# Attention and two MLP layers on one core: rows of maxima read in 8-byte runs, and another step table for the attention

## Chip, cores and metric

The kernel runs on one core of a Trainium2 chip. The metric is the device time of one execution in microseconds (us). TensorE (PE) does the matrix products, its weight loads are listed as PEld; VectorE (DVE), ScalarE (ACT) and GpSimd (POOL) do the work on elements; SyncE (SP) issues nearly all DMAs.

## What is computed

```
q, k, v: (batch 2, heads 8, seq 1152, dim 64) f32
q_pool = q.reshape(B, H, 576, 2, 64).mean(axis=3)
scores = (q_pool @ k^T) / 8 ;  scores -= max over keys
attn   = exp(scores) / (sum over keys + 1e-9)
x      = (attn @ v)  ->  1152 tokens of 512
x      = mish(x @ moe_w_in) @ moe_w_out        # 512 -> 2048 -> 512
out    = elu(x @ moe2_w_in) @ moe2_w_out       # 512 -> 2048 -> 512
```

The four weight matrices come as 64-bit floats; the kernel makes a high and a low 32-bit part of each piece of them.

## The kernel before

**Two stages.** `attention()` goes first, `mlps()` second. The order of all instructions is written out by hand, engine by engine; each engine runs its own list in order, and semaphores hold it where an operand or a buffer is not ready.

**Pairs and units.** The 16 (batch, head) combinations go as eight pairs `n`, the two heads of a pair on partitions 0 to 63 and 64 to 127. The 576 pooled queries of a head are cut in a narrow unit (`c` = 0, queries 0 to 255) and a wide unit (`c` = 1, queries 256 to 575). The 1152 keys are nine key tiles `kt` of 128. One unit and one key tile make one step, so a pair has 18 steps: 0 to 8 for the narrow unit, 9 to 17 for the wide one.

**What a step does.** `qk` (L353 to L366) computes the scores of one key tile, keys on the partitions, queries along the row, for both heads at once: four terms of two matmuls each. Three are products of high and low parts of q and k (`QH`, `QL`, `KH`, `KL`), the fourth (`top`, `unit`) subtracts the query's maximum, held as a row in `tops`. `exp` (L372) on ACT turns the two PSUM banks of scores into `pt`. With a `kt` in the list `two`, two key tiles of the narrow unit share one pair of banks and one ACT instruction of 1024 columns. The score banks are a ring of three double banks, taken in turn by `qk` and by the maxima.

**Maxima.** The maximum of each query is needed ahead of its pair's steps. `peak_mm` (L270 to L293) multiplies with queries on the partitions (L279; L286 for the last 128 keys of all four query tiles; L293 for the last 64 queries of both heads, out of `blk`), `peak` (L295 to L309) reduces each result on DVE, and `top` negates the maxima into `neg`. This is a column with one query per partition. To become a row it goes out to DRAM (`top_out`, L336, tensor `hopm`) and back (`top_in`, L342 and L347) in two parts: first queries 0 to 255, then the rest. Each read of L342 fetches 256 single floats. Only pair 0 takes another way: `flip` transposes on PE (L321).

**Sums and values.** `av` (L443) multiplies a key tile of `pt` with V, a matmul on 128 rows and 64 columns per head, and adds up nine key tiles per unit in one bank. `add` (L383) adds key tiles of `pt` on DVE or POOL, by the table `who`; `total` (L398) sums over the keys with a matrix of ones, one source for each of two tiles of added `pt` and one for each key tile that nobody added. The sums are spilled (L409), go through DRAM (`hop`, L415 and L419), are inverted (L423), come back broadcast over partitions (`pop`, `rb`, L427 and L433), and scale the unit's result (L460), which is split in `XH` and `XL`.

**The table.** `PLAN`, for the last pair `LAST`, and `PREP` for the next pair's loads and maxima give the step of each action: `av` the step of each of the 18 V tiles of a pair (counted from the pair's first step, so a value of 18 or more falls in the next pair), `total` and `chain` the sums, `add` the distance of an addition from its score step. Inside a step the order is: maxima marked even, `qk` and `exp`, maxima marked odd, then `av` with `total`, then ACT, DVE, POOL and SP actions. `weight` gives the steps at which one piece of the first four weight chunks is read and taken apart during each pair; its last action, `rest` (L145), makes the low part.

**MLP stage.** `h_mm` (L178) and `out_mm` (L736) alternate on PE for the rest of the run. The first six units of `h_mm` need tokens of batch 0 only, that is of pairs 0 to 3.

Of the kernel before, what the change touches and what calls it, by code (L numbers as in the profile page):

```python
# [22 lines left out]
def tile_pool_attention_mish_elu_mlp(  # L23
# [20 lines left out]
    P = 128  # L44
# [138 lines left out]
    def attention():  # L183
        with ExitStack() as st:
# [84 lines left out]

            def peak_mm(n, e):  # L270
                t, j = evs(n)[e]
                kw = 512 if n else KB
                if e == 0:
                    stat[n] = ap.tile([P, NQ + 1, 2, 3], F32, tag="stat", name="stat")
                    neg[n] = ap.tile([P, NQ + 1, 2], F32R, tag="neg", name="neg")
                pt = sc[n, e] = take()
                if t < NQ:
                    for h in range(2):
                        nc.tensor.matmul(  # L279
                            pt[:, h, :kw], qh[n][half[h], t * P:(t + 1) * P], kh[n][half[h], j * kw:(j + 1) * kw],  # L280
                            start=True, stop=True,
                        )
                elif t > NQ:
                    for x in range(NQ):
                        for h in range(2):
                            nc.tensor.matmul(  # L286
                                pt[:, h, x * P:(x + 1) * P], qh[n][half[h], x * P:(x + 1) * P], kh[n][half[h], S - P:],
# [23 lines left out]
            def top(n, t0, t1):  # L311
                m, g = stat[n], neg[n] if n else pad[:, :, :, 0]
                nc.vector.tensor_reduce(g[:, t0:t1, :], m[:, t0:t1], axis=AX.X, op=ALU.max, negate=True)
                if t1 == NQ:
                    nc.vector.tensor_reduce(g[:, t1, 0:1], m[:, t1, 0:1], axis=AX.X, op=ALU.max, negate=True)


            def flip(t0, t1):
# [6 lines left out]
                if t0 < NQ:  # L325
                    nc.scalar.copy(tops[0][:, t0 * P:t1 * P], pt[:, :(t1 - t0) * P])
# [4 lines left out]
            def top_out(n, t0, t1):  # L331
                if t0 == 0:
                    hops[n] = dp.tile([P, NQ + 1, 2], F32, tag="hopm", name="hopm")
                e = slice(2 * t0, 2 * t1 + (t1 == NQ))
                hop, g = (x.rearrange("p t h -> p (t h)")[:, e] for x in (hops[n], neg[n]))
                nc.sync.dma_start(out=hop, in_=g.bitcast(F32))  # L336

            def top_in(n, t0, t1):
                hop, row = hops[n], tops[n % 2]
                for h in range(2):  # L340
                    r = h * D
                    nc.sync.dma_start(  # L342
                        out=row[r:r + 1, t0 * P:t1 * P].rearrange("o (t p) -> o t p", p=P).bitcast(F32),
                        in_=hop[:, t0:t1, h].rearrange("p t -> t p").unsqueeze(0),
                    )
                    if t1 == NQ:
                        nc.sync.dma_start(  # L347
                            out=row[r:r + 1, NQ * P:].bitcast(F32), in_=hop[half[h], NQ, 0:1].rearrange("p o -> o p")
                        )
# [25 lines left out]
            ADDS = {1: (0, 0, 1), 3: (1, 2, 3), 4: (0, None, 4), 5: (1, None, 5), 6: (0, None, 6), 7: (1, None, 7)}  # L375
# [99 lines left out]
            def at(s, e, f, *args):  # L475
# [6 lines left out]
                "load_q": [-30, -23],  # L482
                "load_k": [-20, -19],
                "load_v": [-1, 9],
                "pool_q": -20,
                "high_q": -17,
                "high_k": [-17, -15],
                "blk_q": -8,
                "low_q": -9,
                "low_k": [-13, -2],  # L490
                "peak": [-28, -23, -20, -18, -12, -10, -10, -1, 2, 4],
                "top": [[2, 1], [1, 3]],
            }
            PREP[2] = {
                "load_q": [-24, -22],
                "load_k": [-20, -18],
                "load_v": [-3, 0],
                "pool_q": -20,
                "high_q": -18,
                "high_k": [-19, -15],  # L500
                "blk_q": -13,
                "low_q": -13,
                "low_k": [-9, -3],
                "peak": [-28, -24, -23, -19, -11, -10, -9, -1, 1, 4],
                "top": [[2, 1], [1, 3]],
# [376 lines left out]
```

## Time and profile before

| | us |
|---|---|
| median of 3 runs | 634.15 (634.05 to 636.31) |
| profiled execution, its own time | 635.57 |
| span of that execution | 633.8 |
| PE busy | 616.9 (97%) |
| DVE busy | 445.9 (70%) |
| ACT busy | 335.1 (53%) |
| POOL busy | 197.9 (31%) |

The profile gives one execution. Its span runs from the first to the last instruction on the core; the execution's own time is 1.8 us longer, and the median lies 1.4 us below that. Shares of busy time are averages over two stages: POOL is busy for 6.0 of 10 us in most of the attention and hardly at all later.

### The profile page before, as it was taken

What the parts mean: (1) busy time and instruction counts of PE and PEld (TensorE: products, weight loads), DVE (VectorE), ACT (ScalarE), POOL (GpSimd) and SP (SyncE); (2) the same over time, 40 slices, a digit from 0 to 9 for tenths busy, and PEclk for the clock granted to TensorE, in tenths of its full rate; (3) what the DMA queues carried; (4) which work ended last, traced back from release to release, by engine and by line L of the source; (5) the groups of instructions that cost most, each with busy time, mean ns of one, the idle gap of its engine ahead of it and who ended that gap; (6) DMA issues with size and microseconds to landing.
All of it is one profiled execution on the core that took longest, in us unless ns stands there. A gap on an engine that the chain in (4) does not pass through costs nothing.

```text
span 633.8 us, 11509 instructions
## 1 busy us (share of the span) xinstructions
PE 616.9 (97%) x4498; PEld 535.2 (84%) x4498; DVE 445.9 (70%) x705; ACT 335.1 (53%) x675; POOL 197.9 (31%) x191
## 2 busy tenths in 40 slices
PE   5899999999999999999999999999999999999997
PEld 3667676676776689999999999999999999999995
DVE  5868767787787468647548657759878788995453
ACT  3665546555565544434344553456666657664441
POOL 5666565657653511101104323333210101100000
PEclk9999999999999999999999999999999999999999
DMA  4234252442523425223232222222232223300111
GB/s 140 84 99 123 67 134 60 131 111 66 132 64 89 89 76 176 67 67 104 68 97 82 85 71 97 97 70 62 72 99 68 66 68 100 109 25 11 40 51 50
DMA packets 50797, 53.34 MB, mean 84 GB/s; under 512 B 17656, under 2 KB 40248, under 8 KB 50744
## 3 DMA queue, kind: packets, MB, share of 16 engines
q1 hardware_dynamic: 50520, 52.29, 28.6%
q8 instruction: 35, 0.57, 0.4%
q10 hardware_dynamic: 224, 0.33, 0.2%
q14 instruction: 18, 0.15, 0.1%
HBM read 50.14 MB, written 2.47 MB: 83 GB/s over the span
## 4 chain that ended last, share of the span: by engine, by line
PE 86%; DMA 6%; DVE 3%; SPq 2%; issue 1%; ACT 1%; DVEq 0%; ACTq 0%
PE banks L178 32%; PE banks L736 31%; PE banks L363 10%; PE banks L443 8%; DMA top<-hopm 3%; PE banks L279 2%; PE banks L398 2%; DVE stat L300 1%; DMA hopm<-neg 1%; PE banks L293 1%; DVE stat L302 1%; DMA kr<-in_k_dram 1%; SPq L342 1%; DMA raw<-in_moe_w_in_dram 1%; DMA qr<-in_q_dram 1%
## 5 line engine op out<-in xcount | busy, mean ns | idle before, releaser
L178 PE MATMUL banks<-XH,wh 128*128 128x384 f32 x384 | 129.5, 337 | 0.0
L178 PE MATMUL banks<-XL,wh 128*128 128x384 f32 x384 | 129.4, 337 | 0.0
L178 PE MATMUL banks<-XH,wl 128*128 128x384 f32 x384 | 129.4, 337 | 0.0
L123 POOL TENSOR_SCALAR wf<-wf 128x512 f32<-128x512 f32 x64 | 43.6, 682 | 256.2 <-ACT wf L119 225.8
L372 ACT ACTIVATE pt<-banks 128x640 f32<-128x640 f32 (+2 forms) x136 | 88.0, 681 | 63.1 <-PE banks L363 62.7
L300 DVE TENSOR_REDUCE stat<-banks 128x2 f32<-128x1024 f32 (+1 forms) x68 | 77.9, 1171 | 13.2 <-PE banks L279 13.0
L443 PE MATMUL banks<-pt,vr 128*64 128x320 f32 (+1 forms) x576 | 79.6, 414 | 0.0
L178 PEld LDWEIGHTS banks<-XH,wh 128*128 128x128 f32 x384 | 72.0, 188 | 2.3 <-issue 0.5
L178 PEld LDWEIGHTS banks<-XL,wh 128*128 128x128 f32 x384 | 72.0, 188 | 1.8
L178 PEld LDWEIGHTS banks<-XH,wl 128*128 128x128 f32 x384 | 72.0, 188 | 0.0
L690 ACT ACTIVATE gh<-banks 128x384 fp32r<-128x384 f32 x48 | 23.7, 493 | 78.7 <-PE banks L178 78.7
L736 PE MATMUL banks<-gh,wl 128*128 128x384 f32 x192 | 64.5, 336 | 0.0
L736 PE MATMUL banks<-gl,wh 128*128 128x384 f32 x192 | 64.5, 336 | 0.0
L736 PE MATMUL banks<-gh,wh 128*128 128x384 f32 x192 | 64.4, 335 | 0.0
L443 PEld LDWEIGHTS banks<-pt,vr 128*64 128x64 f32 x576 | 37.9, 136 | 27.9 <-issue 5.5
L383 POOL TENSOR_TENSOR add<-pt 128x640 f32<-128x640 f32 (+1 forms) x30 | 43.0, 1434 | 52.4 <-ACT pt L372 52.3
L736 PE MATMUL banks<-wh,gl 128*128 128x512 f32 x144 | 56.2, 390 | 0.0
L736 PE MATMUL banks<-wl,gh 128*128 128x512 f32 x144 | 56.2, 390 | 0.0
L736 PE MATMUL banks<-wh,gh 128*128 128x512 f32 x144 | 56.2, 390 | 0.0
L693 DVE TENSOR_TENSOR gl<-g,gh 128x384 fp32r<-128x384 f32 x48 | 31.1, 649 | 34.1 <-ACT g L691 34.1
L383 POOL TENSOR_TENSOR add<-add,pt 128x640 f32<-128x640 f32 (+1 forms) x31 | 47.1, 1521 | 17.9 <-DVE add L383 11.7
L363 PE MATMUL banks<-QH,KH 64*128 64x320 f32 (+1 forms) x288 | 49.8, 332 | 1.2 <-DVE stat L300 0.6
(85 smaller groups left out, 1220.9 us busy)
## 6 DMA issues: line engine op xcount, KB each, us to landing
raw<-in_moe_w_in_dram SPq DMA_DIRECT2D x28, 512.0 KB
raw<-in_moe_w_out_dram SPq DMA_DIRECT2D x28, 512.0 KB
vr<-in_v_dram SPq DMA_DIRECT2D x16, 288.0 KB
qr<-in_q_dram SPq DMA_DIRECT2D x14, 288.0 KB
kr<-in_k_dram SPq DMA_DIRECT2D x7, 384.0 KB
raw<-in_moe_w_in_dram SPq DMA_DIRECT2D x8, 256.0 KB
raw<-in_moe_w_out_dram SPq DMA_DIRECT2D x8, 256.0 KB
out_dram<-part SPq DMA_DIRECT2D x8, 256.0 KB
```

Of the source, the lines that this page charges most:

```text
L123: nc.gpsimd.tensor_scalar(self.f, self.f, HUGE, -HUGE, op0=ALU.min, op1=ALU.max)
L178: nc.tensor.matmul(pt[:, :TB], w[:, kk * P:(kk + 1) * P], x[:, kk, tk], start=(i == 0), stop=(i == len(terms) - 1))
L279: nc.tensor.matmul(pt[:, h, :kw], qh[n][half[h], t * P:(t + 1) * P], kh[n][half[h], j * kw:(j + 1) * kw], start=True, stop=True,)
L300: nc.vector.tensor_reduce(m[:, t, :, j], pt[:, :, :kw], axis=AX.X, op=ALU.max)
L363: nc.tensor.matmul(pt[:, h, t * w:(t + 1) * w], x[half[h], k0:k0 + P] if x is not None else unit[half[h], :], y[half[h], cols], start=(i = ...
L372: nc.scalar.activation(pts[n, c][:, kt:kt + m], sc.pop((n, c, kt)), AF.Exp, scale=SCALE)
L383: eng.tensor_tensor(d, d if i is None else p[:, i], p[:, j], op=ALU.add)
L398: nc.tensor.matmul(pt[32 * g:32 * (g + 1), :w], ones[:, :32], x[:, h, z * w:(z + 1) * w], start=(i == 0), stop=(i == len(srcs) - 1), tile_ ...
L443: nc.tensor.matmul(acc[n, c][half[h], :w], vs[n][:, h, kt, :], pts[n, c][:, kt, h, :], start=(kt == 0), stop=(kt == KT - 1),)
L690: nc.scalar.activation(gh, h, AF.Mish)
L693: nc.vector.tensor_tensor(gl, g, gh, op=ALU.subtract)
L736: nc.tensor.matmul(pt, l, r, start=(first and i == 0), stop=(final and i == 2))
```

## The change

The maxima are now laid out so that neighbouring queries share a partition. `rows` picks as the weight operand of `peak_mm` every second query of a 256-query block, so partition p of the even tile holds query 2p and that of the odd tile query 2p+1. `neg` and `hopm` become flat, two floats of one head next to each other, and `top_in` reads both heads in one transfer of runs of two floats, and the last 64 queries of both heads in a second one.

```diff
+            def rows(n, h, t):
+                x = qh[n][half[h], t // 2 * 2 * P:(t // 2 + 1) * 2 * P]
+                return x.rearrange("d (p t) -> d t p", t=2)[:, t % 2]
...
-                            pt[:, h, :kw], qh[n][half[h], t * P:(t + 1) * P], kh[n][half[h], j * kw:(j + 1) * kw],
+                            pt[:, h, :kw], rows(n, h, t), kh[n][half[h], j * kw:(j + 1) * kw],
...
-                hop, row = hops[n], tops[n % 2]
-                for h in range(2):
-                    r = h * D
-                    nc.sync.dma_start(
-                        out=row[r:r + 1, t0 * P:t1 * P].rearrange("o (t p) -> o t p", p=P).bitcast(F32),
-                        in_=hop[:, t0:t1, h].rearrange("p t -> t p").unsqueeze(0),
-                    )
...
+                hop, row = hops[n], tops[n % 2].rearrange("(h d) s -> h d s", h=2)[:, 0].bitcast(F32)
+                nc.sync.dma_start(
+                    out=row[:, t0 * P:t1 * P].rearrange("h (p t) -> h p t", t=2),
+                    in_=hop[:, 2 * t0:2 * t1].rearrange("p (h t) -> h p t", h=2),
+                )
+                if t1 == NQ:
+                    nc.sync.dma_start(out=row[:, NQ * P:], in_=hop[:, 2 * NQ:].rearrange("(h j) o -> h (j o)", h=2))
```

The table is another one, with one more entry, `FIRST`, for pair 0. The narrow unit's key tile 8 is now added too, so its sum has two sources; the wide unit's keeps three. Two other moves: `low_q` goes from POOL to DVE, and `rest` of the attention's eight weight pieces from DVE to POOL.

```diff
-                "av": [13, 13, 13, 13, 17, 17, 17, 17, 17, 19, 19, 19, 22, 24, 24, 26, 26, 26],
+                "av": [10, 10, 17, 17, 17, 17, 17, 17, 17, 22, 22, 22, 22, 26, 26, 26, 26, 28],
-                "two": [4],
+                "two": [0, 2, 4, 7],
-                    at(s0 + prep["low_q"], "pool", low_q, n, nc.gpsimd)
+                    at(s0 + prep["low_q"], "rest", low_q, n, nc.vector)
...
-                            f()
+                            f() if f != w.rest else f(nc.gpsimd)
```

The instructions that move stand as follows. From L270 on line numbers are a few higher in the changed kernel (L279 becomes L284, L363 L364, L443 L444, L398 L399, L342 L345).

PE before, in the wide unit of a middle pair, behind its fourth score tile: the maxima of the last 128 keys, the narrow unit's sum with three sources, one group of maxima, the next score tile.

```order
L286 MATMUL banks<-KH,QH 128x128 x8
L398 MATMUL banks<-pt,ones 32x128 x4
L398 MATMUL banks<-add,ones 32x128 x8
L279 MATMUL banks<-KH,QH 128x512 x2
L363 MATMUL banks<-QH,KH 128x320 x2
L363 MATMUL banks<-QH,KL 128x320 x2
L363 MATMUL banks<-QL,KH 128x320 x2
L363 MATMUL banks<-top_83,unit 128x320 x2
```

The same place now, right behind the maxima of the last 128 keys (which follow the second score tile): the last V tile of the pair before, two V tiles of this pair's narrow unit, then scores, and the narrow unit's sum.

```order
L444 MATMUL banks<-pt,vr 64x320 x2
L444 MATMUL banks<-pt,vr 64x256 x4
L364 MATMUL banks<-QH,KH 128x320 x2
L364 MATMUL banks<-QH,KL 128x320 x2
L364 MATMUL banks<-QL,KH 128x320 x2
L364 MATMUL banks<-top_83,unit 128x320 x2
L284 MATMUL banks<-KH,QH 128x512 x2
L364 MATMUL banks<-QH,KH 128x320 x2
L364 MATMUL banks<-QH,KL 128x320 x2
L364 MATMUL banks<-QL,KH 128x320 x2
L364 MATMUL banks<-top_83,unit 128x320 x2
L399 MATMUL banks<-add,ones 32x128 x8
```

Three V tiles of two units now stand in one run, and the sum has lost the source that came straight from `pt`. Over a pair V stood in runs of 4 and 5 (narrow) and 3, 1, 2, 3 (wide) key tiles; it now stands in runs of 7, 4, 4 and of 1 with the next unit's 2, and the run of 7 is followed at once by the maxima of L293.

SP before, in the second half of a wide unit: the column of the first maxima goes out, three loads follow, then the two reads of the row, then the narrow unit's sum (`hop`, `tot`).

```order
L336 DMA hopm<-neg 128x4
L233 DMA qr<-in_q_dram 128x576
L109 DMA raw<-in_moe_w_in_dram 128x4x128
L239 DMA vr<-in_v_dram 128x576
L342 DMA top_85<-hopm 1x256x1 x2
L415 DMA hop<-sum 4x128
L226 DMA kr<-in_k_dram 128x768
L419 DMA tot<-hop 128x4
```

SP now, same place:

```order
L341 DMA hopm<-neg 128x4
L434 DMA rb<-pop 64x320 x2
L416 DMA hop<-sum 4x128
L226 DMA kr<-in_k_dram 128x768
L420 DMA tot<-hop 128x4
L345 DMA top_85<-hopm 2x128x2
```

The read of the row is one transfer instead of two, and it has moved behind both hops of the narrow unit's sum.

POOL before, from the narrow unit's first additions to the wide unit's last, of one pair:

```order
L383 TENSOR_TENSOR add<-pt 128x2x256 x2
L249 TENSOR_TENSOR QL<-qr,QH 128x576
L383 TENSOR_TENSOR add<-add,pt 128x2x256 x2
L383 TENSOR_TENSOR add<-pt 128x640
L259 TENSOR_TENSOR KL<-kr,KH 128x384
L383 TENSOR_TENSOR add<-pt 128x640
L243 TENSOR_TENSOR qr<-qr 128x576
L383 TENSOR_TENSOR add<-add,pt 128x640 x2
```

POOL now:

```order
L384 TENSOR_TENSOR add<-pt 128x2x256
L145 TENSOR_TENSOR wl<-wf,wh 128x512
L384 TENSOR_TENSOR add<-pt 128x2x256
L384 TENSOR_TENSOR add<-add,pt 128x2x256 x4
L384 TENSOR_TENSOR add<-pt 128x640
L243 TENSOR_TENSOR qr<-qr 128x576
L123 TENSOR_SCALAR wf<-wf 128x512
L384 TENSOR_TENSOR add<-pt 128x640
L384 TENSOR_TENSOR add<-add,pt 128x640 x3
```

POOL has eleven additions per pair where it had eight, and a weight's low part; `QL` is gone from it.

## Rows read from the trace of the kernel before

**Rows 1.** Waits of PE's matmuls, 20 to 230 us: total, times, longest.

```profile
PE banks L363 <- DMA top<-hopm: 2.2, 4, 0.8
```

**Rows 2.** Chain that ended last, in order of time: start, length, what.

```profile
76.75 2.75 DMA top<-hopm
...
139.63 5.76 DMA top<-hopm
...
228.00 8.52 PE banks L178 x48
```

**Rows 3.** Timeline of PE (start, length): first score matmuls of five wide units.

```profile
25.73 0.42 PE L363 MATMUL banks<-QH,KH 64*128 64x320 f32 x2 [0.16 <-DVE stat L300]
...
78.23 0.41 PE L363 MATMUL banks<-QH,KH 64*128 64x320 f32 x2
...
106.64 0.41 PE L363 MATMUL banks<-QH,KH 64*128 64x320 f32 x2
...
132.40 0.41 PE L363 MATMUL banks<-QH,KH 64*128 64x320 f32 x2
...
185.44 0.41 PE L363 MATMUL banks<-QH,KH 64*128 64x320 f32 x2
```

**Rows 4.** Timeline of PE around V runs (L443) and around maxima without V.

```profile
101.95 0.40 PE L279 MATMUL banks<-KH,QH 64*128 64x512 f32 x2
102.28 1.30 PE L443 MATMUL banks<-pt,vr 128*64 128x320 f32 x8
103.50 0.39 PE L363 MATMUL banks<-QH,KH 64*128 64x256 f32 x2
103.73 0.28 PE L363 MATMUL banks<-QH,KL 64*128 64x256 f32 x2
...
104.88 1.84 PE L443 MATMUL banks<-pt,vr 128*64 128x320 f32 x12
...
124.90 0.40 PE L279 MATMUL banks<-KH,QH 64*128 64x512 f32 x2
125.13 0.28 PE L363 MATMUL banks<-QH,KH 64*128 64x256 f32 x2
125.25 0.28 PE L363 MATMUL banks<-QH,KL 64*128 64x256 f32 x2
```

**Rows 5.** Timeline of PE: the narrow unit's sum, one source, then two.

```profile
109.64 0.43 PE L398 MATMUL banks<-pt,ones 128*32 128x128 f32 x8
109.89 0.62 PE L398 MATMUL banks<-add,ones 128*32 128x128 f32 x16
```

**Rows 6.** ACT groups by form, 26 to 228 us: busy, mean ns | idle before.

```profile
L372 ACT ACTIVATE pt<-banks 128x640 f32<-128x640 f32 x72 | 46.3, 706 | 37.9 <-PE banks L363 37.9
...
L119 ACT ACTIVATE wf<-raw 128x512 f32<-128x512 f32 x8 | 5.6, 698 | 0.3
...
L409 ACT ACTIVATE sum<-banks 128x128 f32<-128x128 f32 x8 | 2.2, 278 | 2.5 <-PE banks L398 2.4
```

**Rows 7.** POOL and DVE groups by form, 26 to 228 us.

```profile
L383 POOL TENSOR_TENSOR add<-add,pt 128x640 f32<-128x640 f32 x16 | 27.9, 1746 | 4.7 <-ACT pt L372 4.0
...
L383 POOL TENSOR_TENSOR add<-add,pt 128x512 f32<-128x512 f32 x14 | 17.9, 1279 | 12.1 <-DVE add L383 11.7
...
L249 POOL TENSOR_TENSOR QL<-qr,QH 128x576 fp32r<-128x576 f32 x6 | 11.4, 1892 | 0.0
...
L259 DVE TENSOR_TENSOR KL<-kr,KH 128x768 fp32r<-128x768 f32 x6 | 5.7, 949 | 0.0
```

**Rows 8.** Timeline of SP's queue: start, length of the issue.

```profile
76.08 0.63 SPq L342 DMA_DIRECT2D top<-hopm  x1
...
124.79 0.52 SPq L415 DMA_DIRECT2D hop<-sum  x1
...
127.09 0.52 SPq L419 DMA_DIRECT2D tot<-hop  x1
```

**Rows 9.** One stretch: length, busy of PE, PEld, DVE, ACT, POOL, granted clock, DMA share, GB/s.

```profile
130.40:131.40 1.00, 1.00 (x10) 0.48 (x8) 0.65 (x1) 1.00 (x3) 1.00 (x1) 1.00 0.11 1
```

More of the change, by code (lines that the diff above doesn't have):

```diff
@@ L481, in attention @@
             PREP[1] = {
[L482 to L492, printed above, removed]
+                "load_q": [-53, -41],
+                "load_k": [-36, -26],
@@ L498, in attention @@
[L498 to L505, printed above, removed]
+                "load_q": [-29, -29],
+                "load_k": [-22, -20],
+                "load_v": [-5, 2],
+                "pool_q": -25,
+                "high_q": -20,
+                "high_k": [-21, -19],
@@ L511, in attention @@
-                "total": [12, 20],
-                "chain": [[0, 1, 4, 6, 7, 9, 11, 12, 13, 18], [0, 1, 1, 3, 4, 5, 8, 11, 14, 15]],
-                "two": [4],
-                "weight": [7, 9, 12, 12, 14, 14, 15, 7],
+                "who": [{1: 0, 3: 0, 4: 0, 5: 0, 6: 0, 7: 0, 8: 1}, {1: 0, 3: 0, 5: 1, 7: 0, 4: 0, 6: 0}],
+                "add": [{1: 3, 3: 4, 4: 3, 5: 3, 6: 4, 7: 1, 8: 1}, {1: 1, 3: 1, 4: 4, 5: 3, 6: 3, 7: 2}],
+                "av": [10, 10, 17, 17, 17, 17, 17, 17, 17, 22, 22, 22, 22, 26, 26, 26, 26, 28],
@@ new lines, in attention @@
+                "total": [13, 21],
+                "chain": [[-1, 1, 1, 2, 5, 5, 9, 12, 13, 13], [-1, 1, 1, 3, 5, 6, 11, 13, 14, 17]],
+                "two": [0, 2, 4, 7],
+                "weight": [3, 6, 7, 10, 15, 16, 17, 5],
+            }
+            FIRST = {
+                "who": [{1: 0, 3: 0, 4: 1, 5: 0, 6: 0, 7: 0, 8: 0}, {1: 0, 3: 1, 5: 1, 7: 0, 4: 0, 6: 0}],
+                "add": [{1: 2, 3: 1, 4: 4, 5: 3, 6: 2, 7: 1, 8: 3}, {1: 2, 3: 2, 4: 4, 5: 1, 6: 3, 7: 1}],
+                "av": [10, 10, 17, 17, 17, 17, 17, 17, 17, 22, 22, 22, 22, 26, 26, 26, 26, 28],
+                "total": [13, 21],
+                "chain": [[-1, 1, 2, 4, 5, 7, 11, 12, 13, 13], [-1, 1, 2, 4, 6, 9, 11, 12, 14, 16]],
@@ L523, in attention @@
-                "early": [0, 21, 20],
+                "who": [{1: 0, 3: 1, 4: 1, 5: 1, 6: 1, 7: 1, 8: 0}, {1: 0, 3: 1, 5: 1, 7: 1, 4: 1, 6: 1}],
+                "add": [{1: 5, 3: 4, 4: 3, 5: 4, 6: 5, 7: 2, 8: 1}, {1: 2, 3: 1, 4: 5, 5: 1, 6: 4, 7: 1}],
+                "av": [10, 10, 10, 18, 20, 20, 20, 20, 21, 24, 25, 25, 25, 25, 25, 25, 25, 26],
+                "total": [15, 22],
+                "chain": [[-1, 1, 1, 1, 5, 8, 10, 12, 13, 13], [-1, 1, 1, 2, 5, 5, 11, 12, 13, 15]],
+                "weight": [2, 6, 8, 8, 17, 20, 26, 5],
```

62 lines of the change are left out of this document (31 added, 31 removed).

## Prediction

> **What bounds the kernel now.** I read the chain that ended last first. From 228.00 us [rows 2] it is matmuls of the MLP stage without a break to the end, and the change touches nothing there: it can only move the moment at which that stage begins. So I take the attention apart, in PE's timeline. One period runs from a wide unit's first score matmul to the next pair's. The calmest takes 132.40 - 106.64 = 25.76 us [rows 3], with PE waiting for nobody. The six periods from 25.73 to 185.44 take 159.71, that is 5.15 more than six calm ones, and one of them alone (78.23 to 106.64) takes 28.41. So the attention is PE's own work, plus waits of 0.86 us per pair on average, of which rows of maxima that come late are a part (2.2 us on the matmuls [rows 1], the biggest releaser there). To gain much, a change must shorten PE's work; to lose, it must add waits.
>
> **PE's work: changes of kind.** What a run of V tiles costs is seen in [rows 4]. A run of two lasts 1.22 us from start to start (102.28 to 103.50), a run of three 1.76 (104.88 to 106.64 [rows 3]), so a tile is 0.54 and 0.14 belongs to the run. The maxima's matmuls ahead of it take 0.33 (101.95 to 102.28) where the same ones between scores take 0.23 (124.90 to 125.13): 0.10 more. The first score term behind it takes 0.23 where it takes 0.12 elsewhere (125.25 - 125.13): 0.11 more. A run costs 0.14 + 0.10 + 0.11 = 0.35, two changes of kind on PE (64-row scores to 128-row V and back) at 0.175 each.
>
> Per middle pair V stood in six runs and stands in four: four changes fewer. V now borders on L293's matmuls and on L286's, one change fewer each, and the narrow sum no longer borders on L286's, one more. Five fewer in all, 0.88 us. Counted through PE's whole list from the first wide unit to the MLP stage, where the first and the last pair save less, it is 33 changes: 33 x 0.175 = **5.8 us**. Thirteen of the borders that remain (V beside L293 or L286) stand nowhere in the trace; I price each as one change and let it lie between nothing and 0.35: plus or minus 2.3.
>
> **The narrow sum.** A source takes 0.25 us (109.64 to 109.89 [rows 5]); eight pairs lose one each: **2.0 us**. Its price lies off PE: an eighth addition for DVE, whose load falls all the same (two additions per pair less, one more, the weight's low part gone, `QL` come: by columns 949 x 576/768 = 712 ns [rows 7]).
>
> PE's work falls by 7.8 us, between 5.5 and 10.1. The matmuls of scores, maxima and V are the same in number.
>
> **New waits.** Three places have become tighter, each worked out on PE's time within a middle pair.
>
> First, ACT in the wide unit. `pt` of the wide unit has one buffer, so its first `exp` waits for the lone ninth V tile of the pair before, which now stands behind two score tiles and L286. From the end of that tile PE has two narrow V tiles, six score tiles at 0.59 (four terms at 0.147), two groups of maxima and the sum ahead of the ninth score tile, some 6.2 us with the changes. That score tile needs the seventh `exp` done. ACT needs 7 x 0.706 + 0.698 + 0.278 = 5.92 us [rows 6] from the same moment, and follows PE by about a tenth. Nothing to 1.0 us per pair; I take 0.5, since the score tiles in between wait for the two latest `exp`s in the same way.
>
> Second, the first part of the row. `top_in` is one transfer instead of two but stands behind both hops of the narrow sum. The hop out takes 2.3 us from issue to the next hop's (124.79 to 127.09 [rows 8]). Counted from the narrow unit's start, PE has 16.8 us of work up to the sum and 1.2 with it and the next score tile; that tile's `exp` (0.71) and the spill (0.28) follow, so the spill ends at about 19.1; plus 2.3 and 0.5 for the next issue, the read of the row goes out at about 22.0, takes 0.63 to issue [rows 8] and 2.75 to land, as one read of 256 floats does now [rows 2]: 25.4, against a need at about 25.1, where the next narrow unit's first tile reaches its fourth term. The 0.5 of the first place shifts the need by as much, so 0.2 is left. Alone it would be 0.3 or, with loads in the way, up to 2.
>
> Third, POOL. It loses `QL` (1.89 us) and gets two narrow additions (2 x 1.28), one wide (1.75) [rows 7] and a weight's low part (about 1.28, taken as another two-input operation on 512 columns): 3.7 more per pair. Counted through its list with these durations, its last wide addition ends some 1.2 us before the wide sum needs it. Nothing to 0.5; I take 0.2.
>
> That is 0.9 per pair, between 0 and 3, in place of 0.86 now: no gain and no loss in the six periods, and I add 0.8 us for the two outer pairs, which have the same squeeze on ACT. What goes to nothing: the six fewer ACT instructions of narrow `exp`s per pair and the shorter SP queue lie beside PE's work; the transfers saved (three per pair on SP) are covered by the same place. The head to 25.73 has the same matmuls and the same reductions in another order; I leave it as it is, with 1.5 either way, about half of what the worst period has over the calm one. At the MLP's start the last pair's scaling is covered by six units that need batch 0 only; without that cover it would be a wait of a few us, once.
>
> **Sum.** 7.8 - 0.8 = 7.0. The profiled execution's 635.57 would become 628.6; the median of the three runs lies 1.4 below, 634.15 becomes **627.1**.
>
> **The step of two floats.** The weight operand of L284 and L291 is now read at every second float. No instruction of PE in this trace reads its weights so. A score term's two loads and two matmuls together take 0.12 us [rows 4], so a load is worth at most 0.06; I take the step at nothing, the other end is a rival. [...]
>
> **Rivals.**
> Fewer waits: today's 5.15 us have single causes (the 28.41 period has 2.65 of them), and a table with everything earlier may drop most. At 0.2 per pair instead of 0.86 over six periods it is another 4.0 plus the 0.8 that I added: 622.3. For it: half the runs in the rows' reads. Against it: the three places above.
> The gain eaten: waits of 1.7 per pair over seven pairs, from ACT's seven `exp`s at the full 1.0 and a row 0.7 late. 0.8 x 7 = 5.6 lost: 632.
> Slower, the row late: if the single read of 8-byte runs takes as long as the two reads do now (5.76 us, 139.63 [rows 2]), it lands 3.0 us later than reckoned, 2.4 after the shift, in seven pairs: 17 us against 7.0, or 644. It decides from 1.0 us of added wait per pair, that is from a read of about 4.3 us. While only such reads were in flight, the DMA share was 0.11 [rows 9], less than two engines of sixteen. [...] Against the rival: a read of 256 runs lands in 2.75 today, and it has 256 runs still.
> Slower, the loads: 192 weight loads of the maxima at 0.06 more, none hidden, are 11.5 us: 639. It decides from 0.036 per load. For it: L291's eight matmuls have little streaming to hide a load behind. Against it: loads overlap with the matmuls ahead.
> That the change does not do what it says: the runs could stay single floats. Then the number of DMA packets would not fall, and the time would be near the row-late case.
>
> **Chances.** As forecast 0.52, own range 624.5 to 630. Fewer waits 0.18. Eaten 0.17. Row late, with the runs that stay single, 0.07. Loads 0.06. Within 0.5% (630.98 to 637.32), about what a measurement of this kernel can tell from no change, lies most of the eaten case. Faster by more: 0.52 + 0.18 + 0.04 = 0.74; same 0.13; slower 0.13. The range leaves out both slower cases and the edge of the others: 621.5 to 633.
>
> **What the changed profile would show.** Right: PE's calm period at 24.6, four V runs per pair, the sum's fence of two sources near 0.5 us, the MLP stage beginning near 221 and lasting as long as now. Wrong in the waits: PE waiting for `exp` in the wide unit by more than 1 us per pair, or for `top` at each narrow unit's first tile. Wrong in the step: L291's eight matmuls longer than L286's are now. Wrong in the price of a change: calm periods away from 24.6 with no waits in them.

## The result, and the profile after

The changed kernel takes 628.63 us (628.05 to 629.87, four runs) against 634.89 (634.05 to 636.31, four runs) beside it on the same chip: a ratio of 0.9896, interval 0.9875 to 0.9918. Forecast were 627.1 us and a range of 621.5 to 633. The profiled execution has a time of its own of 629.87 us and a span of 627.9, where before it had 635.57 and 633.8.

The periods first, as in [rows 3]: the timeline of PE of the changed kernel (start, length), the first score matmul of five wide units and the MLP stage's first matmul.

```profile
26.72 0.36 PE L364 MATMUL banks<-QH,KH 64*128 64x320 f32 x2
...
77.29 0.41 PE L364 MATMUL banks<-QH,KH 64*128 64x320 f32 x2
...
102.80 0.42 PE L364 MATMUL banks<-QH,KH 64*128 64x320 f32 x2
...
128.29 0.42 PE L364 MATMUL banks<-QH,KH 64*128 64x320 f32 x2
...
179.38 0.42 PE L364 MATMUL banks<-QH,KH 64*128 64x320 f32 x2
...
222.17 0.45 PE L178 MATMUL banks<-XH,wh 128*128 128x384 f32 x1
```

The six periods from 26.72 to 179.38 take 152.66 where they took 159.71: 7.05 less. They are all alike now, 25.1 to 25.6; no period of 28.41 is left. The first one begins 0.99 later (26.72 against 25.73). The seventh lost 0.47 more, and the stretch from the last wide unit to the MLP stage grew by 0.77 (17.62 to 18.39). The MLP stage lasts 405.7 of the span, before 405.9 (from its first matmul at 227.93). So 7.05 + 0.47 - 0.99 - 0.77 + 0.14 is the 5.9 by which the span fell.

Next what PE waits for, 20 to 230 us, as in [rows 1] (total, times, longest); all its rows in the changed kernel:

```profile
PE banks L399 <- DVE add L384: 0.9, 1, 0.9
PE banks L364 <- DVE stat L305: 0.7, 2, 0.4
PE banks L364 <- ACT pt L373: 0.3, 1, 0.3
PE banks L284 <- ACT pt L373: 0.2, 1, 0.2
```

No wait for a row of maxima is left, nor is a read of one left on the chain of work that ended last, of which [rows 2] shows two. The weight loads of PE do wait. These are the two largest of their rows with an engine as releaser:

```profile
PEld banks L364 <- ACT pt L373: 6.0, 15, 1.0
...
PEld banks L284 <- DVE stat L305: 3.4, 11, 0.5
```

Last the two prices that [rows 5] and the forecast's last paragraph speak of: L291's eight matmuls with their new weight operand, then the sum with two sources (timeline of PE, changed kernel).

```profile
104.07 0.58 PE L291 MATMUL banks<-KH,QH 64*128 64x128 f32 x8
104.58 0.75 PE L444 MATMUL banks<-pt,vr 128*64 128x320 f32 x3
...
107.84 0.64 PE L399 MATMUL banks<-add,ones 128*32 128x128 f32 x16
108.41 0.42 PE L364 MATMUL banks<-QH,KH 64*128 64x320 f32 x2
```

L291 takes 0.51 from start to start. The sum takes 0.57; before, its three sources lasted from 109.64 to the next matmul, 0.80:

```profile
110.44 0.50 PE L279 MATMUL banks<-KH,QH 64*128 64x512 f32 x2
```

The gain is 0.23 where [rows 5] gave 0.25.

### The profile page after: what moved, and what is told of

Its sections match the earlier page's. It is cut to its first block, busy times and chain, and to the rows that moved or that the text cites. A ratio compares the mean times of both kernels' runs of the same rounds, so it can differ in the third digit from the quotient of the medians.

```text
span 627.9 us, 11285 instructions
## 1 busy us (share of the span) xinstructions
PE 613.0 (98%) x4434; PEld 533.7 (85%) x4434; DVE 447.2 (71%) x694; ACT 333.9 (53%) x652; POOL 224.2 (36%) x210
## 4 chain that ended last, share of the span: by engine, by line
PE 92%; DVE 3%; DMA 2%; SPq 1%; issue 1%; ACT 0%; DVEq 0%
PE banks L178 32%; PE banks L744 31%; PE banks L364 12%; PE banks L444 10%; PE banks L284 3%; PE banks L399 2%; DVE stat L305 2%; PE banks L298 1%; DMA rb<-pop 1%; DMA qr<-in_q_dram 1%; PE banks L291 0%; SPq L239 0%; DVE add L384 0%; DMA tot<-hop 0%; DVE part L769 0%
## 5 line engine op out<-in xcount | busy, mean ns | idle before, releaser
L123 POOL TENSOR_SCALAR wf<-wf 128x512 f32<-128x512 f32 x64 | 44.3, 693 | 252.7 <-ACT wf L119 222.2
L384 POOL TENSOR_TENSOR add<-add,pt 128x512 f32<-128x512 f32 (+1 forms) x50 | 77.0, 1552 | 12.1 <-DVE add L384 8.9
L444 PE MATMUL banks<-pt,vr 128*64 128x320 f32 (+1 forms) x576 | 76.7, 411 | 0.0
L444 PEld LDWEIGHTS banks<-pt,vr 128*64 128x64 f32 x576 | 38.6, 136 | 27.6 <-issue 3.5
L128 DVE TENSOR_SCALAR wf<-wf 128x512 int32<-128x512 int32 x64 | 45.5, 712 | 18.8 <-POOL wf L123 18.8
L724 ACT CAST gh<-g 128x384 fp32r<-128x384 f32 x48 | 24.7, 514 | 48.2 <-DVE g L718 47.9
```

Of the source, the lines that this page charges most:

```text
L123: nc.gpsimd.tensor_scalar(self.f, self.f, HUGE, -HUGE, op0=ALU.min, op1=ALU.max)
L128: nc.vector.tensor_scalar(f, f, 3, None, op0=ALU.logical_shift_left)
L384: eng.tensor_tensor(d, d if i is None else p[:, i], p[:, j], op=ALU.add)
L444: nc.tensor.matmul(acc[n, c][half[h], :w], vs[n][:, h, kt, :], pts[n, c][:, kt, h, :], start=(kt == 0), stop=(kt == KT - 1),)
L724: nc.scalar.copy(gh, g)
```

## Experiments: the new reading alone

The theory behind the forecast: the table brings nearly all of the gain through PE's work, and the reading is worth its row's direct waits at most. The rival: the reading takes away more than is listed as waiting for it.

**The reading with the old table.** `rows`, `top`, `flip`, `top_out` and `top_in` as in the change, table and sum as before:

```diff
+            def rows(n, h, t):
...
-                for h in range(2):
-                    r = h * D
-                    nc.sync.dma_start(
...
+                nc.sync.dma_start(
+                    out=row[:, t0 * P:t1 * P].rearrange("h (p t) -> h p t", t=2),
```

> The kernel before with the new way of reading the maxima alone (weights at every second float, one transfer of 8-byte runs for both heads), the table as before. Theory (PE's work makes the gain, the reading only takes waits away): PE's own work is unchanged, a calm period stays at 25.8 us; the waits of score matmuls for the row, 2.2 us in all, mostly go, because the row lands 2 to 3 us earlier: 1 to 3 us faster than before. Rival (the reading is the larger part of the gain): 4 to 6 us faster. Rival (weights at every second float load slower): slower than before, and the eight matmuls of the last 128 keys take more than 0.5 us.

Measured: 630.5 us (629.94 to 630.68) against 635.12, ratio 0.9924 (0.9909 to 0.9938). That is 4.6 us for the reading alone. Timeline of PE of this kernel, three wide units:

```profile
103.95 0.41 PE L364 MATMUL banks<-QH,KH 64*128 64x320 f32 x2
...
129.70 0.41 PE L364 MATMUL banks<-QH,KH 64*128 64x320 f32 x2
...
155.44 0.41 PE L364 MATMUL banks<-QH,KH 64*128 64x320 f32 x2
```

Every middle period is 25.74 to 25.75, the calm one of [rows 3]. All 5.15 us that lay above six calm periods are gone, and 0.9 of it is given back in the head. The same is seen in one row of a view that sums the stretch from 30 to 210 us (length, then busy time of PE, PEld, DVE, ACT and POOL with counts, granted clock, DMA share, GB/s). First the kernel before:

```profile
30.00:210.00 180.00, 177.07 (x1965) 124.28 (x1961) 136.46 (x202) 100.68 (x191) 105.02 (x77) 1.00 0.38 97
```

Then the reading alone:

```profile
30.00:210.00 180.00, 180.00 (x2051) 127.47 (x2045) 140.32 (x206) 104.09 (x198) 108.72 (x80) 1.00 0.39 101
```

PE stood idle for 2.93 us before and for none with the new reading. So a good half of the 5.15 was idle time of PE; the rest lay inside matmuls that count as busy. Nearly half of the idle time is one wait in the long period of 28.41, and the row is not its direct cause. Timelines of the kernel before (SP, then ACT, then PE):

```profile
85.73 3.37 SPq L342 DMA_DIRECT2D top<-hopm  x2
...
90.23 0.38 SPq L226 DMA_DIRECT2D kr<-in_k_dram  x1
...
95.16 0.83 ACT L256 CAST KH<-kr 128x768 fp32r<-128x768 f32 x1 [4.67 <-DMA kr<-in_k_dram]
...
96.54 0.50 PE L279 MATMUL banks<-KH,QH 64*128 64x512 f32 x2 [1.33 <-ACT pt L372]
```

The row's reads held SP for 3.37 us, the load of k behind them went out late, ACT waited 4.67 us for it, and the `exp` behind that cast came 1.33 us late for PE. With the new reading the same load goes out 5.3 us behind the row's way out instead of 6.5, the cast follows it by 3.2 instead of 4.9, and ACT's waits for k fall from 19.5 us in all to 9.7.

**As many transfers as before.** The kernel of the last experiment, each read cut into one transfer per head:

```diff
-                nc.sync.dma_start(
-                    out=row[:, t0 * P:t1 * P].rearrange("h (p t) -> h p t", t=2),
-                    in_=hop[:, 2 * t0:2 * t1].rearrange("p (h t) -> h p t", h=2),
-                )
+                for h in range(2):
+                    nc.sync.dma_start(
+                        out=row[h:h + 1, t0 * P:t1 * P].rearrange("h (p t) -> h p t", t=2),
+                        in_=hop[:, 2 * t0 + 2 * h:2 * t0 + 2 * h + 2].unsqueeze(0),
+                    )
```

> The kernel before with the new reading alone (old table), and each read of the row cut into one transfer per head, so four transfers of 128 runs of 8 bytes per pair instead of two of 256: as many runs, as many transfers as in the kernel before. My theory: SP is held by the number of runs, so the time stays at that of the reading alone, 630.5, with all middle periods at 25.74. Rival: what holds SP is the number of transfers; then waits of up to 0.86 us per pair come back, the periods are uneven again, and the time goes back to 633 to 635.

Measured: 630.7 us (629.77 to 631.74), ratio 0.9931 (0.9918 to 0.9944), middle periods 25.76 to 25.77. The number of transfers does not matter here. What this kernel shares with the last one, and the kernel before lacks, is half as many runs, of 8 bytes; the order of the weights, which they share too, moves no period (see the step of 8 bytes below). The issue on SP is not what decides: here the two reads, which held SP for 3.06 us before (from 113.13), pass in 1.16 (timeline of SP of this kernel),

```profile
110.06 1.16 SPq L346 DMA_DIRECT2D top<-hopm  x2
111.32 0.55 SPq L417 DMA_DIRECT2D hop<-sum  x1
```

and in the reading alone the one read passes in 0.54, but the issue behind it takes 2.87:

```profile
110.40 0.54 SPq L345 DMA_DIRECT2D top<-hopm  x1
111.03 2.87 SPq L416 DMA_DIRECT2D hop<-sum  x1
```

The time is the same with both.

**Which transfer was late.** In the kernel before, the loads of k stand behind the row's reads in SP's queue, and ACT waits for them for 19.5 us in all. To tell the late k from the late row I put k ahead, from the third pair on; nothing moves on any other engine (`low_k` changes its step, but not its place in POOL's list):

```diff
-                "load_k": [-20, -18],
+                "load_k": [-22, -22],
...
-                "low_k": [-9, -3],
+                "low_k": [-9, -5],
```

> The kernel before, old reading and old table, but from the third pair on the two loads of k stand ahead of the row's reads in SP's queue (steps -22 and -22 instead of -20 and -18); nothing moves on the other engines. My theory: what the slow reads cost besides the rows that PE waits for (2.2 us) is that k's loads stand behind 3 to 4 us of reads; with k ahead, ACT's waits for kr fall from 19.5 us in all to under 8, the period from 78 to 106 falls from 28.41 to 26.5 or less, and the time goes from 635.1 to 632 or 633. The row itself comes some 0.9 us later, which can give back up to 1 us. Rival: k is not what was late; the row alone is, the waits for it grow from 2.2 us, and the time stays at 635 or goes up by 1 to 4 us.

Measured: 647.68 us (644.51 to 650.17), ratio 1.0198 (1.0171 to 1.0225). ACT's waits for k fell to 0.9 us, as meant, and the time went up by 12 us. The rival had the sign right, and its size by a factor of three too small. The queue of SP in this kernel, the row's way out and its read:

```profile
118.82 0.33 SPq L336 DMA_DIRECT2D hopm<-neg  x1
...
121.62 4.08 SPq L342 DMA_DIRECT2D top<-hopm  x2
```

The read starts 2.80 us after the way out instead of 1.86 (111.27 to 113.13), and takes 4.08 to issue instead of 3.06. PE then stands at the row (waits of PE, 20 to 250 us):

```profile
PE banks L363 <- DMA top<-hopm: 8.6, 14, 1.2
```

That is 6.4 more than in [rows 1], of 12 lost. Another part is the clock. The same kind of row as above, for two stretches of this kernel behind two such waits:

```profile
42.00:48.00 6.00, 6.00 (x53) 3.50 (x56) 2.73 (x5) 2.16 (x4) 2.58 (x3) 0.72 0.03 3
...
102.00:108.00 6.00, 6.00 (x70) 3.80 (x66) 3.19 (x7) 1.96 (x5) 1.67 (x2) 0.83 0.09 28
```

In the six us ahead of each of them PE was busy for 4.45 and 4.90 only (granted clock 1.00 and 0.89), and then the granted clock is 0.72 and 0.83 of full speed on average. Behind another such stretch (154 to 160 us, busy for 4.43 of 6) it reads 1.00, so what lowers it is not shown. In the kernel before, the clock reads 1.00 in every stretch that was read from 20 to 185 us. What each part cost to the microsecond I did not separate.

So with single floats the row leaves hardly any room: put later, it costs PE 6.4 us in direct waits alone. The run does not show that k was on time: it moved two transfers at once, k earlier and the row later, and in the kernel before a late k did reach PE once, through ACT (the 1.33 us above). Half as many runs in the reads took both waits away.

**The table with the old reading.** The changed kernel, its reading functions as before:

```diff
-                            pt[:, h, :kw], rows(n, h, t), kh[n][half[h], j * kw:(j + 1) * kw],
+                            pt[:, h, :kw], qh[n][half[h], t * P:(t + 1) * P], kh[n][half[h], j * kw:(j + 1) * kw],
```

> The changed kernel with the old way of reading: two reads of 256 single floats, weights unstrided; the new table stays. Theory (the new table needs the shorter read, since the row now stands behind both hops of the narrow sum): the second read goes out about 0.6 us later and two together need up to 5.8 us where one needs 2.8, so the first narrow tile waits 1 to 3 us for its row in each of seven pairs: 7 to 20 us slower than the changed kernel, that is no faster than before. Rival (the reading is independent of the table): within 2 us of the changed kernel.

Measured: 632.39 us (630.53 to 633.86), ratio 0.9953 (0.9937 to 0.9969). Both expectations missed: it is 3.8 us slower than the changed kernel, and in the profiled execution, the fastest of the six, no row is late but once (waits of PE, 20 to 230 us):

```profile
PE banks L363 <- DMA top<-hopm: 0.9, 1, 0.9
```

Two of its six periods are long, 26.38 and 26.78 (the second with this wait), and the others are 25.1 to 25.7, as in the changed kernel. So the new table alone also frees most of the rows, and no read of one holds SP for more than 1.19 us there, where before it was up to 3.16. What the slower executions of this kernel waited for is not known.

The two halves of the change give 4.6 and 2.7 alone and 6.3 to 6.5 together: they overlap by about 1 us.

## Experiments: PE's work

**The price of a change of kind.** The run of seven V tiles of the middle pairs and of pair 0 is cut into four and three, two changes more per pair:

```diff
-                "av": [10, 10, 17, 17, 17, 17, 17, 17, 17, 22, 22, 22, 22, 26, 26, 26, 26, 28],
+                "av": [10, 10, 16, 16, 16, 16, 17, 17, 17, 22, 22, 22, 22, 26, 26, 26, 26, 28],
```

> The changed kernel with the run of seven V tiles cut in four (a step earlier) and three, in seven pairs: nothing is added but 14 changes of kind on PE. Theory (a change costs 0.175 us): 14 x 0.175 = 2.4 us slower, periods of 25.85 us instead of 25.5, less by up to 0.2 per pair if the pause lets ACT catch up in the wide unit. Rival (runs of V cost nothing by themselves, and the gain came from waits): no change, or faster.

Measured: 630.55 us (630.19 to 630.96), ratio 0.9925 (0.9912 to 0.9938). The middle periods are 25.80, 0.30 above the changed kernel's 25.50: 0.15 for a change, where the forecast took 0.175 from [rows 4]. The two slow score tiles described in the next section last as long there (0.72 and 0.76), so no relief elsewhere hides in the price.

**The price of a source.** The narrow unit's last key tile is not added, in all three tables; the entry of the middle pairs:

```diff
-                "who": [{1: 0, 3: 0, 4: 0, 5: 0, 6: 0, 7: 0, 8: 1}, {1: 0, 3: 0, 5: 1, 7: 0, 4: 0, 6: 0}],
+                "who": [{1: 0, 3: 0, 4: 0, 5: 0, 6: 0, 7: 0}, {1: 0, 3: 0, 5: 1, 7: 0, 4: 0, 6: 0}],
```

> The changed kernel, but the last key tile of the narrow unit is again not added, so that its sum has three sources as in the kernel before. My theory: L398's matmuls of the narrow unit take 0.80 us instead of 0.57, every period from wide unit to wide unit grows from 25.5 to 25.73, and the time goes up by 8 x 0.23 = 1.8 us to 630.5. Rival: the addition that this source spares DVE or POOL relieves the new waits (about 0.9 us per pair), the periods stay at 25.5 or fall, and the time is 628.5 or less.

Measured: 630.48 us (629.99 to 630.87), ratio 0.9926 (0.9914 to 0.9938); middle periods 25.71 to 25.77, 0.24 above. The price holds, and the addition that DVE or POOL saves relieves nothing.

**The step of 8 bytes.** The maxima's weights are 128 neighbouring queries again, with the row read as in the change; so each maximum lands beside another query, and the kernel serves for its time alone.

```diff
-                x = qh[n][half[h], t // 2 * 2 * P:(t // 2 + 1) * 2 * P]
-                return x.rearrange("d (p t) -> d t p", t=2)[:, t % 2]
+                return qh[n][half[h], t * P:(t + 1) * P]
```

> The changed kernel, but the weight operand of the maxima is 128 neighbouring queries again instead of every second one; the row is still read in runs of 8 bytes, so each maximum stands beside another query of the same block and the scores are shifted by the wrong amount. My theory: the step of 8 bytes in the weight operand costs nothing (eight matmuls of L291 take 0.51 us as L286's before), so the time stays at 628.6 within 0.5 and the periods at 25.5. Rival (strided weight loads): the narrower operand is hidden nowhere but I cannot see it in PE's rows, since loads lie beside matmuls; then it is worth 1 us or more per pair, and the time falls by 3 to 11 us.

Measured: 627.69 us (627.58 to 628.28), ratio 0.9885 (0.9872 to 0.9898). The middle periods are the same to 0.02 us (25.49, 25.51, 25.49), so the step costs the periods nothing; but the time is 0.9 lower. The intervals of the two ratios overlap, so it is the trace that shows it: the first wide unit starts 1.3 earlier (25.40), the MLP stage 2.1 earlier (220.04). Most of the difference lies in the head. With the new order a tile of queries holds every second one of 256, so the first maximum of pair 0 needs the second half of q as well. The first two rows of PE in the changed kernel:

```profile
6.11 1.33 PE L284 MATMUL banks<-KH,QH 64*128 64x384 f32 x6 [6.11 <-ACT QH L246]
7.85 0.69 PE L284 MATMUL banks<-KH,QH 64*128 64x384 f32 x2 [0.41 <-DVE stat L305]
```

Before, the first two matmuls started as soon as k was there:

```profile
4.69 0.69 PE L279 MATMUL banks<-KH,QH 64*128 64x384 f32 x2 [4.69 <-ACT KH L256]
```

**Pair 0 in the old order.** Its row goes through PE and never through DRAM, so it needs no new order:

```diff
             def rows(n, h, t):
+                if n == 0:
+                    return qh[n][half[h], t * P:(t + 1) * P]
```

with `flip` copying straight, as before.

> The changed kernel, but pair 0, whose row goes through PE and not through DRAM, keeps the old order of queries in its maxima (weight operand of 128 neighbouring queries, row copied straight). My theory: the head is longer since the first maximum of pair 0 now needs both loads and both casts of 128 queries; with the old order the first matmul starts at 4.7 to 5.5 us instead of 6.11, the first wide unit at 25.4 instead of 26.7, the periods stay at 25.5, and the time is 1.3 us less than the changed kernel, 627.3. Rival: the longer head comes from the new table (other steps of FIRST and PREP[1]), and the time stays at 628.6.

Measured: 627.76 us (626.75 to 627.93), ratio 0.9879 (0.9859 to 0.9899). The head is as before and the periods as in the changed kernel (first row of PE, this kernel):

```profile
4.66 0.69 PE L286 MATMUL banks<-KH,QH 64*128 64x384 f32 x2 [4.66 <-ACT KH L256]
```

The first wide unit begins at 25.89, the middle periods are 25.51 to 25.54. The head's 0.99 was the order of the queries and not the table; the reading alone shows the same lateness (26.59).

## Experiments: the new waits in the wide unit

By the two prices just measured the table saves 5 x 0.15 + 0.24 = 0.99 us per pair. Against the reading alone the period fell from 25.74 to 25.50 only. So 0.75 us per pair are left over, by these prices, for new waits, and they do not show as idle time of PE. In the period from 128.29 two score tiles in a row last 0.73 and 0.75 us from start to start instead of 0.59, and the maxima behind them 0.34 instead of 0.23. That is 0.41 of the 0.75; the rest I do not find in single rows. The place in the timeline of the changed kernel, ACT, PEld and PE:

```profile
134.80 0.71 ACT L373 ACTIVATE pt<-banks 128x640 f32<-128x640 f32 x1 [0.29 <-PE banks L364]
134.83 0.30 PE L364 MATMUL banks<-QH,KH 64*128 64x320 f32 x2
...
135.56 0.19 PEld L364 LDWEIGHTS banks<-QH,KH 64*128 64x128 f32 x2 [0.26 <-ACT pt L373]
135.56 0.41 PE L364 MATMUL banks<-QH,KH 64*128 64x320 f32 x2
...
136.31 0.19 PEld L284 LDWEIGHTS banks<-KH,QH 64*128 64x128 f32 x2 [0.16 <-DVE stat L305]
...
136.65 0.30 PE L364 MATMUL banks<-QH,KH 64*128 64x320 f32 x2
```

The load at 135.56 waits for the `exp` that ends at 135.51, and that `exp` had waited 0.29 for PE. Scores and maxima take the ring's three double banks in turn; with no V run between them a tile's bank is not yet empty when its turn comes. That is read from these rows; no run changed the ring. Four experiments looked for a way around it.

**Make the `exp`s start earlier.** The lone ninth V tile of the wide unit goes two steps forward, in pair 0 as well:

```diff
-                "av": [10, 10, 17, 17, 17, 17, 17, 17, 17, 22, 22, 22, 22, 26, 26, 26, 26, 28],
+                "av": [10, 10, 17, 17, 17, 17, 17, 17, 17, 22, 22, 22, 22, 26, 26, 26, 26, 26],
```

> The changed kernel with the lone ninth V tile of the wide unit two steps earlier, in one run with the four tiles ahead of it, so that the first exp of the next wide unit no longer waits for a V tile behind its second score tile. The number of changes of kind on PE is the same. Theory (what is left of waits in a period is mostly ACT held by that buffer): periods fall from 25.5 to about 25.0 us, 3 to 4 us faster than the changed kernel. Rival (ACT's own work in the wide unit, or the reductions on DVE, is the limit): periods stay within 0.15 us.

Measured: 629.92 us (629.59 to 630.24), ratio 0.9915 (0.9900 to 0.9929). The periods went up, to 25.70 (one is 26.06), and the two slow tiles last 0.95 and 0.90. The waits for `exp` shrank (from 6.0 us of PEld to 1.4) and those for DVE's reductions grew (3.4 to 7.9). Timeline of DVE and POOL of this kernel:

```profile
131.71 1.56 POOL L384 TENSOR_TENSOR add<-pt 128x640 f32<-128x640 f32 x1 [0.33 <-ACT pt L373]
...
132.59 1.49 DVE L259 TENSOR_TENSOR KL<-kr,KH 128x768 fp32r<-128x768 f32 x1
...
133.23 2.14 POOL L243 TENSOR_TENSOR qr<-qr 128x576 f32<-128x576 f32 x1
134.01 1.21 DVE L305 TENSOR_REDUCE stat<-banks 128x2 f32<-128x1024 f32 x1
```

With the earlier `exp` POOL's addition comes earlier too, and DVE's `KL` meets it: 1.49 us instead of the 0.95 of [rows 7]. It holds POOL's next instruction in turn (2.14, before 1.44) and delays a reduction, which PE then waits for.

**The same with `KL` out of the way.** On top of the plain pair 0, the lone tile as above and `KL` ahead of the reduction of L309:

```diff
-                "low_k": [-8, -15],
+                "low_k": [-9, -15],
```

> The kernel of e9 (pair 0 plain) with the lone ninth V tile two steps earlier, as in e4, and from the third pair on DVE's low part of k (KL, 768 columns) ahead of the reduction of L309 instead of behind it, where in e4 it ran beside a POOL addition in 1.49 us instead of 0.95. My theory: e4 failed only by that meeting of DVE and POOL; with KL out of the way the exponentials of the wide unit start earlier and PE no longer waits for them, the periods fall from 25.5 to 25.2 and the time from 627.8 to 625.7. Rival: the reduction behind KL is now late, or POOL's addition of 128x640 meets the next instructions of DVE; the periods go to 25.7 as in e4 and the time to 629.

Measured: 627.11 us (626.81 to 628.12), ratio 0.9872 (0.9849 to 0.9895). The periods are 25.40. This `KL` is at 0.95 again (timeline of DVE):

```profile
128.48 0.95 DVE L259 TENSOR_TENSOR KL<-kr,KH 128x768 fp32r<-128x768 f32 x1
```

So the meeting of DVE and POOL was what turned the earlier tile into a loss (25.70 against 25.40). The gain is a third of the 0.3 per pair that was expected, and in the same place a tile still takes 0.76 (134.50 to 135.26), with an `exp` ahead of it that again waits 0.29 for PE. The score tiles of the wide unit did not get shorter at all (nine of them take 6.16 in this kernel and in the changed one); the 0.1 lies in the V tiles, which in their new runs take 3.85 instead of 3.94. So the theory that the earlier `exp`s free PE fell here too.

**Take a copy out of ACT's list there.** The first action on each weight chunk's piece (L119, 0.70 us) stands among the wide unit's `exp`s. On top of the plain pair 0:

```diff
-                "weight": [3, 6, 7, 10, 15, 16, 17, 5],
+                "weight": [3, 6, 10, 13, 18, 19, 20, 2],
```

> The kernel of e9 with, beside it, each weight chunk's piece started three steps earlier (step 2 of a pair instead of 5), so that ACT's first copy of it stands ahead of the wide unit's exponentials (step 8) and not among them (step 11); all later actions on the piece but one stay at their step. My theory: ACT's 0.6 us for this copy delays two exponentials of each wide unit, on which PE then waits 0.3 us; the periods fall from 25.5 to 25.2 and the time by 2 us against e9, to 625.3. Rival: the exponentials of the wide unit are limited elsewhere (PE's scores, the ring of three banks), the periods stay at 25.5 and the time at that of e9.

Measured: 627.7 us (627.2 to 628.16), ratio 0.9881 (0.9861 to 0.9900): the time without it. The periods fell by 0.08, not by 0.3, and the two slow tiles still last 0.72 and 0.77. ACT's copy is not what the tiles wait for; the rival holds.

**The same action later**, with the two that follow it (L123 on POOL, L128 on DVE). The numbers of `weight` are ages of one piece, one for each of its actions, counted from the step that stands last; the expectation below takes them for steps and the actions for pieces of a chunk:

```diff
-                "weight": [3, 6, 7, 10, 15, 16, 17, 5],
+                "weight": [3, 11, 12, 14, 15, 16, 17, 5],
```

> The changed kernel, but the pieces 2, 3 and 4 of each weight chunk are read and taken apart at steps 11, 12 and 14 of each pair instead of 6, 7 and 10. My theory: part of the 0.9 us of new waits per pair in the wide unit is ACT, which makes copies for these pieces ahead of exponentials; elsewhere in the pair they cost nothing, the PEld waits of L364 on ACT fall from 6.0 us in all to under 4, periods fall from 25.5 to 25.1, and the time to 625.5. Rival: what limits there is the rate of ACT's exponentials as such, or another engine takes over the wait; the periods stay at 25.5 within 0.1 and the time at 628.6 within 0.7.

Measured: 638.67 us (637.99 to 639.85), ratio 1.0057 (1.0044 to 1.0069), 10 us slower than the changed kernel; periods 27.5 (one is 28.10). Neither side expected that. Timeline of DVE and POOL of this kernel:

```profile
148.12 0.61 POOL L123 TENSOR_SCALAR wf<-wf 128x512 f32<-128x512 f32 x1 [3.92 <-ACT wf L119]
148.69 3.07 POOL L384 TENSOR_TENSOR add<-add,pt 128x640 f32<-128x640 f32 x2
...
152.43 1.03 DVE L133 SCALAR_TENSOR_TENSOR wf<-raw,wf 128x512 int32<-128x512 int32 x1
153.49 1.66 DVE L134 SCALAR_TENSOR_TENSOR wf<-raw,wf 128x512 int32<-128x512 int32 x1
155.08 3.47 DVE L305 TENSOR_REDUCE stat<-banks 128x2 f32<-128x1024 f32 x3
```

POOL waits 3.92 us at the head of its list for ACT's copy, with the additions behind it, and PE's sum waits 0.83 for the last of them at 151.82. On DVE the three weight instructions now stand ahead of three reductions, which pile up, and PE waits 0.63 for one at 157.47. In this period the sum lasts 1.03 longer than in the changed kernel and the maxima ahead of 157.47 0.79 longer, nearly all of the 2.0 lost. So the place of three short instructions cost 10 us, three times the 3.1 that was hoped for.

## Why the prediction was right

**The sum.** Forecast 7.0 us less, measured 6.3 by the medians (5.9 by the spans). The six periods were to be 24.6 + 0.9 = 25.5 each, and they are 25.5. The head was 0.99 longer, inside the 1.5 allowed, and for a reason that the diff could have told: the forecast looked at the matmuls and reductions of the head and not at which half of q the first one now needs. The 0.8 added for the outer pairs came out as 0.8 in the last stretch and a gain of 0.5 in the seventh period. That last stretch hangs on one wait: the 0.9 of L399 above, an addition on DVE behind a scaling that waits 1.51 us for its broadcast. In the kernel with pair 0 plain it is not there, and the stretch is 17.37 instead of 18.39. With the reading alone it is 16.45, so that the new table costs the last pair another 0.9 that no run here explains.

**PE's work.** The mechanism and both prices hold: 0.15 for a change where 0.175 was taken, 0.23 to 0.24 for a source where 0.25 was. With them the 33 changes and eight sources make 6.8 us where the forecast had 7.8, inside its 5.5 to 10.1. The forecast's sign of a wrong price, calm periods away from 24.6 with no waits in them, would have misled: PE shows no wait in periods of 25.5, the prices hold all the same, and what lies above 24.6 sits inside matmuls that count as busy. That the step of two floats would cost nothing was the forecast's own estimate, which no row of the kernel before shows; the rival of strided loads is out by the periods, the second to the fourth of which take 25.49 to 25.51 with the step and without it. L291's eight matmuls take 0.50 to 0.51 us from start to start with it and 0.48 to 0.49 without it, in the same table.

**The waits: equal in number, not in kind.** This is the step that was right by luck of cancellation. The forecast set 0.9 new against 0.86 old per pair. The old 0.86 fell to the reading alone, 4.6 us net and 5.1 in the periods, which the forecast had priced at nothing beyond the row ("the shorter SP queue lie beside PE's work"). The new waits came with the table, some 0.75 per pair by the measured prices. Of the three places named, the first is the one. By the trace it is not ACT's seven `exp`s at their rate, since ACT itself waits there and its copies make no difference, but the ring of three banks, which the forecast has only in the half sentence on the score tiles in between; no run changed the ring. The row (second) is not late at all, and the new waits of POOL (third) do not show.

**The rivals.** Row late: its point of decision was right in kind, since in the run with k ahead a row read 0.9 us later costs PE 6.4 us more in direct waits, with single floats (12 us in all, the clock among them). But with runs of 8 bytes PE waits for no row, and two heads in one transfer do no harm, since one transfer per head takes as long (630.7 against 630.5). That the change doesn't do what it says is out: DMA packets fell from 50797 to 46975. Fewer waits and gain eaten each happened in one half of the change: the reading alone lost all idle time between 30 and 210 us, the table alone was eaten to 2.7 us.

## What to carry to other kernels

Before a gain is credited to a new order, run the other half of the change alone: here 4.6 of 6.3 us are to be had by halving the runs of a small DMA on a path with no slack. An instruction moved off one engine's crowded stretch can drag its followers on other engines along, and those can cost more than the stretch gives (10 us for an expected gain of 3). A slow issue in a queue delays what stands behind it (SP was held for 3.37 us, and ACT waited 4.67 for the load behind), so a late load of k can be the row's doing. And look for waits where PE counts as busy: a tile that lasts 0.75 instead of 0.59 us holds a wait that no idle time shows.

The run with the plain pair 0, the earlier lone tile and `KL` ahead is the fastest here, 627.11 us, ratio 0.9872 to the kernel before; against the changed kernel's 0.9896 it was not timed side by side, and the intervals overlap.

## What the hardware showed

**DVE and POOL held each other up here.** The shift of L128 on DVE takes 0.40 us in the kernel before and 1.52 in the changed one where it starts under a POOL addition (groups by form of the kernel before, 26 to 228 us; then timeline of POOL and DVE, changed kernel):

```profile
L128 DVE TENSOR_SCALAR wf<-wf 128x512 int32<-128x512 int32 x8 | 3.2, 399 | 2.0 <-POOL wf L123 2.0
```

```profile
135.85 1.56 POOL L384 TENSOR_TENSOR add<-pt 128x640 f32<-128x640 f32 x1
...
136.17 1.52 DVE L128 TENSOR_SCALAR wf<-wf 128x512 int32<-128x512 int32 x1
```

It ends at 137.69, 0.28 after the addition. The reductions of 1024 columns, which read PSUM, take 1.21 to 1.23 with or without POOL beside them. The `KL` and `qr` above (1.49 for 0.95, 2.14 for 1.44) show it in both directions: `KL` ends 0.81 behind POOL's addition, and `qr` 1.29 behind `KL`. What the two engines share is not shown.

**The reads of single floats landed late and unevenly.** Those of 256 stand on the chain of the kernel before with 4.75, 2.75, 5.76, 5.00 and 2.81 us, and with k ahead nine times, with 2.69 to 5.84; with runs of 8 bytes none stands on it in the changed kernel, with the reading alone or with one transfer per head. What holds SP at an issue (0.54 us for one read of a row, 4.08 for two, or 2.87 for the issue behind one) I did not settle.
